# Three experts' token rows transposed by VectorE instead of TensorE, low-part products last, one conversion job moved

## The chip, the core and the metric

The kernel runs on one core of one Trainium2 chip. The metric is the device time of one execution in microseconds (us); the lower the better. Every number of the trace below comes from one profiled execution of the kernel before.

## The reference

Three layers in a row, on 2 sequences of 768 tokens with 512 features.

```python
def reference(**kwargs):
    attn_out = _attn_ref(**attn_kwargs)        # 8 heads of 64, window of 96 earlier tokens + 8 global ones, ALiBi bias
    x = attn_out.transpose(0, 2, 1, 3).reshape(B, S, H * D)
    x = _moe_ref(x=x, **moe_kwargs)            # 8 experts, each token goes to one
    return _moe2_ref(x=x, **moe2_kwargs)       # trigonometric token mixing

# expert layer, for each token: e is chosen (the gate may keep the expert of the token before it), p is a softmax of the logits
    h = np.maximum(x[b, s] @ w1[e], 0.0)       # w1: 8 x 512 x 1024
    out[b, s] = p[e] * (h @ w2[e])             # w2: 8 x 1024 x 512

# last layer
    theta = x @ w_theta
    zr, zi = x * np.cos(theta), x * np.sin(theta)
    y = np.einsum('ts,bsd->btd', w_tok_r, zr) + np.einsum('ts,bsd->btd', w_tok_i, zi)
    u = x + y
    return u + np.maximum(u @ w_ch, 0.0)
```

## The kernel before

The program is scheduled by hand: each engine executes its instructions in the order in which the Python code issues them, and an instruction that has to wait holds up all that stands behind it on its engine.

**Stages.** Attention fills the first 112 us of the span, the eight experts go from 112 to 288 us, the last layer takes the rest. The experts are sorted by their number of tokens; `r` is the place in that order. Expert `r` has room for `RCAP[r]` tokens (288, 256, 240, 208, 192, 176, 160, 144), in one tile of 128 and a remainder. The hidden width of 1024 is cut into 8 parts of 128; the loop variable `u` = 8r + f runs over all 64 parts.

**Matrix products in two parts.** Most float32 operands are split into a high part and a remainder, both in the type fp32r, and a product is made of three: high x high, high x low and low x high. The splits are made by ScalarE (the high copy, L1486 for w2, L1369 for w1) and VectorE (the subtraction, L1487, L1370). For `r` >= 4 (192 tokens or fewer, `FEW`) the first product (`mm1`, L1505) takes unsplit float32 operands and two parts of the width go together as a pair; its result passes `relu` (L1553 on ScalarE, L1554 and L1555 on VectorE). `mm2` (L1580) is split for all experts: per part `u` and tile `i` it issues hh x h2, hh x l2, hl x h2. The small remainder tiles of `r` >= 4 go through `mm2_few` (L1596). The split parts of w2, `w2s0` and `w2s1`, have three buffers each, so the split of part u + 3 needs the buffer of part u.

**Rows of an expert.** `gather_x` (L1046) fetches the rows of one tile of tokens from DRAM with one indirect DMA on GpSimd's queue, three tiles ahead. `x_tr` turns the tile: four transposes on TensorE (L1341) into PSUM, then a copy by ScalarE for `r` >= 4 (L1344). It is called for both tiles of expert r + 1 while expert r is at f = 2; for `r` >= 4 it stands between `mm1` and `mm2` of that pair. `load_piece` (L1030, L1034) fetches the weights of two parts on SyncE's queue, 512 KB for w1 and 512 KB for w2, three pairs ahead.

**Conversion jobs.** The last layer's weights come as 64-bit floats. A job converts a 128 x 512 piece in six steps, which `job_tick` issues one by one: L418 on ScalarE with L419 on VectorE, then L421, L423, L425 on VectorE, L428 on ScalarE (which also issues the load of a later piece), L431 on VectorE. There are 26 jobs. They are spread over attention, the experts (`tick`, `JRATE` is the rate per expert) and the last layer (two steps at each of three places of a block `k`: `T1`, `T2`, `T3`).

**The last layer** goes block by block of 128 tokens. For block `k` TensorE runs `h_mix(k, 0)`, `h_theta(k + 2)`, `h_mix(k, 1..3)` (L1929 and L1843). Beside it `h_tr(k + 3)` transposes the rows of a later block on VectorE (L1798), `h_xh` and `h_xl` split the result (L1814 on ScalarE, L1827 on VectorE) for `h_theta(k + 3)`, and `trig_a`, `trig_s`, `trig_b`, `trig_c` of block k + 2 make from theta (`th`) the tiles `z` that `h_mix(k + 2)` multiplies: L1853 and L1858 on ScalarE, L1860 to L1864 on VectorE, sines on ScalarE, products with the rows (L1884, L1892) and the split of `z` (L1904 on ScalarE, L1909 on VectorE). Before the loop over `k` the code runs `trig_c(1, hi)`, `h_mix(0, 3)`, then `trig_a`, `trig_s`, `trig_b`, `trig_c` of block 2. At the head of block 1, `job_upto(10)` finishes the job that is under way.

Of the kernel before, what the change touches and what calls it, by code (L numbers as in the profile page):

```python
# [12 lines left out]
I32 = mybir.dt.int32  # L13
# [38 lines left out]
VT = 2  # L52
NRAW = 3
# [21 lines left out]
JRATE = (2.0, 1.2, 1.3, 3.0, 2.7, 2.3, 0.8)  # L75
T1, T2, T3 = 2, 2, 2
# [39 lines left out]
def kernel(  # L116
# [338 lines left out]
    prow = toks.rearrange("p i w e -> p (i w e)")[:, 0:25].bitcast(I32)  # L455
    y0 = ct([128, DM], F32, "y0")
# [554 lines left out]
    def load_piece(n, parts=(1, 2)):  # L1011
# [16 lines left out]
        if 1 in parts:  # L1028
            p[1] = pre.tile([128, 4, 256], F32, tag="raw1", name="raw1", bufs=NRAW)
            SP.dma_start(  # L1030
                p[1], w1[bass.ds(ev, 1), :, c * 256 : (c + 1) * 256].rearrange("o (a p) f -> p (o a) f", p=128)
            )
# [7 lines left out]
    def gather_x(n):  # L1040
# [5 lines left out]
        G.indirect_dma_start(xg[:M], None, xd[:], bass.IndirectOffsetOnAxis(ap=xidx[:M, r, i : i + 1], axis=0))  # L1046
        xgs[n] = xg

# [275 lines left out]

    def x_tr(r, i, low=True):
# [7 lines left out]
        xg = xgs.pop(n)  # L1333

# [4 lines left out]
        M = min(128, RCAP[r] - i * 128)  # L1339
# [47 lines left out]
    with ExitStack() as mctx:  # L1387
# [179 lines left out]
        def mm2(u):  # L1567
            r, f = divmod(u, 8)
            if f == 0:
                yps[r] = [pO.tile([128, DM], F32, tag="o", name="o") for _ in range(RTILES[r] - (r == E - 1))]  # L1570
            h2, l2, w = wsp2.pop(u)
            hh, hl, hx = hts.pop(u)
            fews[u] = hx, w
            for i in range(RTILES[r]):
                lo = i * 128
                M = min(128, RCAP[r] - lo)
                if width(r, i) == 128:
                    out = yps[r][i]
                    for q, (ha, wa) in enumerate(((hh, h2), (hh, l2), (hl, h2))):
                        PE.matmul(  # L1580
                            out[:M],
                            lhsT=ha[:, lo : lo + M],
                            rhs=wa,
                            start=(f == 0 and q == 0),
                            stop=(f == 7 and q == 2),
                        )
# [79 lines left out]
        for u in range(64):  # L1666
# [41 lines left out]
            elif u % 2 == 0:  # L1708
# [7 lines left out]
                mm2(u)  # L1716
                mm2(u + 1)
# [5 lines left out]
                for _ in range(3):  # L1723
                    tick()
                relu(u + 3)
                for _ in range(3):
                    tick()
                split_w2(u + 3)
                if u == SU:
# [11 lines left out]
            if u == 1:  # L1741
                prob_rows()
            if f == (0 if r else 2):
# [21 lines left out]
    with ExitStack() as hctx:  # L1765
# [292 lines left out]
        trig_c(1, hi, V)  # L2058
        h_mix(0, 3)
# [3 lines left out]
        trig_c(2)  # L2063
# [113 lines left out]
```

## Time and profile before

| | |
|---|---|
| time, median of 3 runs | 466.54 us (466.2 to 466.86) |
| time of the profiled execution | 466.93 us |
| its span, first to last instruction | 465.0 us |
| granted TensorE clock over the span | 0.999 |
| TensorE busy | 457.9 us (98%) |
| VectorE, ScalarE, GpSimd busy | 344.0, 262.3, 142.9 us |

The span is what the trace shows; the time holds 1.9 us more around it. Engines are PE (TensorE matmuls), PEld (its weight loads), DVE (VectorE), ACT (ScalarE), POOL (GpSimd) and SP (SyncE). In a timeline each row has a start in us from the span's beginning, a duration in us, the engine, the line of the code, the operation, the tiles written and read, the shape and a count; a bracket tells how long the engine was idle before it and what ended that.

### The profile page before, as it was taken

Reading aid. Unit: us, or ns where it says so; the run is one execution under the profiler, and the core shown is the slowest. Engines: PE = TensorE matmul, PEld = TensorE weight load, DVE = VectorE, ACT = ScalarE, POOL = GpSimd, SP = SyncE. Lnnn points to the kernel's source line nnn. Section 1 sums busy time; section 2 is a strip of 40 time slices with the busy share of each in tenths; the row PEclk is TensorE's granted clock in tenths of the full one; section 3 lists DMA queues with packets and bytes.
Section 4 is the critical chain, followed back from the end, with each engine's and each line's share of the span. In section 5 each row is a group of like instructions: output and inputs, shape, how many; then the busy total and the mean of one; then the engine's idle time right before and its main releaser. Section 6 shows DMA issues by size and latency. Waiting matters only on the chain.

```text
span 465.0 us, 9578 instructions
## 1 busy us (share of the span) xinstructions
PE 457.9 (98%) x3346; PEld 378.7 (81%) x3346; DVE 344.0 (74%) x946; ACT 262.3 (56%) x623; POOL 142.9 (31%) x203
## 2 busy tenths in 40 slices
PE   8999999999999999999999999999999999999996
PEld 4677777788888898888787788888888888888886
DVE  5888889768687697887888776687997897741522
ACT  5988786822456666655755544556765665630300
POOL 8602313204032404040514302654874441000400
PEclk9999999999999999999999999999999999999999
DMA  8978577715957788788999993521253110000022
GB/s 241 367 231 248 184 240 253 252 47 158 356 167 225 265 296 270 257 277 270 318 348 307 305 312 132 165 91 48 79 152 109 43 49 24 0 35 34 28 87 93
DMA packets 61770, 85.60 MB, mean 184 GB/s; under 512 B 6248, under 2 KB 40296, under 8 KB 61720
## 3 DMA queue, kind: packets, MB, share of 16 engines
q1 hardware_dynamic: 52212, 62.06, 40.8%
q0 software_dynamic: 5552, 12.55, 8.8%
q10 hardware_dynamic: 3956, 10.36, 6.6%
q8 instruction: 27, 0.44, 0.4%
q14 instruction: 23, 0.19, 0.1%
HBM read 73.56 MB, written 11.38 MB: 183 GB/s over the span
## 4 chain that ended last, share of the span: by engine, by line
PE 90%; ACT 4%; DVE 3%; issue 1%; DMA 1%; POOL 0%; DVEq 0%
PE a L1929 22%; PE o L1580 15%; PE h L1524 10%; PE h L1505 8%; PE b L1966 7%; PE th L1843 7%; PE s L574 4%; PE x L653 3%; PE o L1596 3%; PE pt L629 3%; ACT pr L606 2%; PE tr L1341 1%; PE y L670 1%; DVE sm L596 1%; ACT ps L638 1%; PE h L783 1%
## 5 line engine op out<-in xcount | busy, mean ns | idle before, releaser
L1929 PE MATMUL a<-wtokr,z 128*128 128x512 f32 x480 | 85.3, 336 | 0.0
L1929 PEld LDWEIGHTS a<-wtokr,z 128*128 128x128 f32 x480 | 74.2, 188 | 10.0
L1580 PE MATMUL o<-w2s,hh 128*128 128x512 f32 x192 | 62.7, 406 | 0.0
L606 ACT ACTIVATE pr<-sm,st 128x256 f32<-128x256 f32 (+1 forms) x96 | 46.0, 483 | 15.3 <-DVE st L596 15.2
L1524 PE MATMUL h<-xT,w1s 128*128 128x288 f32 (+3 forms) x384 | 51.4, 284 | 0.5 <-DVE xT L1347 0.5
L1524 PEld LDWEIGHTS h<-xT,w1s 128*128 128x128 f32 x384 | 48.7, 189 | 3.4 <-issue 0.6
L1783 POOL DMA_INDIRECT xq<-yd,Lall x40 | 42.4, 1059 | 25.2 <-issue 9.8
L1487 DVE TENSOR_TENSOR w2s<-raw,w2s 128x512 fp32r<-128x512 f32 x56 | 38.5, 689 | 8.4 <-ACT w2s L1486 8.4
L596 DVE CUSTOM_DVE_ANT_0 sm<-s,bias 128x256 f32<-128x256 f32 (+1 forms) x96 | 34.0, 395 | 9.2 <-PE s L574 5.1
L1505 PEld LDWEIGHTS h<-xT,raw 128*128 128x128 f32 x256 | 37.0, 190 | 4.4 <-issue 3.9
L1505 PE MATMUL h<-xT,raw 128*128 128x192 f32 (+3 forms) x256 | 40.5, 311 | 0.0
L1580 PE MATMUL o<-w2s,hl 128*128 128x512 f32 x96 | 38.0, 396 | 0.0
L1580 PEld LDWEIGHTS o<-w2s,hh 128*128 128x128 f32 x192 | 32.4, 184 | 5.8 <-DVE w2s L1487 1.0
L1486 ACT ACTIVATE w2s<-raw 128x512 fp32r<-128x512 f32 x56 | 34.8, 626 | 2.9 <-DMA raw<-in_w_dram 1.4
L1635 POOL DMA_DIRECT2D yd<-yo x13 | 8.2, 634 | 79.1 <-ACT yo L1631 72.4
L1974 DVE SCALAR_TENSOR_TENSOR ob<-b,xTf 128x512 f32<-128x512 f32 (+1 forms) x16 | 8.8, 558 | 29.0 <-PE b L1966 25.7
L1370 DVE TENSOR_TENSOR w1s<-raw,w1s 128x512 fp32r<-128x512 f32 x32 | 22.0, 689 | 6.9 <-ACT w1s L1369 6.4
L574 PE MATMUL s<-kall,q 64*128 64x256 f32 (+1 forms) x192 | 26.1, 391 | 0.0
L629 PE MATMUL pt<-ident,pr 128*128 128x128 f32 x176 | 24.6, 278 | 0.2
L653 PE MATMUL x<-ps,vv 128*64 128x128 f32 x352 | 24.5, 279 | 0.0
L428 ACT ACTIVATE wtokr<-jw 128x512 fp32r<-128x512 f32 x15 | 9.5, 633 | 24.6 <-DVE jw L425 24.6
L1843 PE MATMUL th<-wth,xh 128*128 128x512 f32 x88 | 22.4, 396 | 0.0
(294 smaller groups left out, 944.3 us busy)
## 6 DMA issues: line engine op xcount, KB each, us to landing
raw<-in_w_dram SPq DMA_DIRECT2D x60, 512.0 KB, 5.4
vv<-in_pack_dram SPq DMA_DIRECT2D x10, 512.0 KB, 6.5
jraw<-in_w_tokT_dram ACTq DMA_DIRECT2D x10, 512.0 KB, 5.0
w<-in_w_dram SPq DMA_DIRECT2D x16, 256.0 KB, 5.4
kall<-in_pack_dram SPq DMA_DIRECT2D x10, 320.0 KB, 5.3
xd<-xt SPq DMA_DIRECT2D x12, 256.0 KB, 2.3
q<-in_pack_dram SPq DMA_DIRECT2D x11, 256.0 KB, 4.4
jraw<-in_w_tokT_dram ACTq DMA_DIRECT2D x10, 256.0 KB, 4.7
```

The costliest lines, as they stand in the source:

```text
L574: PE.matmul(sp[hh][:, 0:W], lhsT=qs[n][half, j], rhs=kall[half, b, j, t * 160 + 160 - W : t * 160 + 160], start=True, stop=True,)
L596: V.tensor_tensor_reduce(out=sm[:, hh, 0:W], in0=ust[u]["s"][hh], in1=bias[:, 2 * j + hh], scale=-0.125, scalar=BIG, op0=ALU.add, op1=ALU.min,
L606: A.activation(pr[:, hh, 0:W], sm[:, hh, 0:W], AF.Exp, bias=st[:, hh : hh + 1], scale=-1.0, accum_out=sums[n][:, 2 * j + hh : 2 * j + hh + 1],
L629: PE.transpose(pt[:, hh, c], pr[:, hh, c * 128 : (c + 1) * 128], ident)
L653: PE.matmul(xp[64 * hh : 64 * hh + 64, j], lhsT=vv[:, i, h * 64 : (h + 1) * 64], rhs=ps[:, hh, c], start=(c == 0), stop=(c == nch - 1),)
L1487: V.tensor_tensor(l2, bb[:, o], f32(h2), op=ALU.subtract)
L1505: PE.matmul(hp[:, :N], lhsT=pieces[u // 2][1][:, j, o * 128 : (o + 1) * 128], rhs=x[:, j, :N], start=(j == 0), stop=(j == 3),)
L1524: PE.matmul(hp[:, :N], lhsT=wa[:, j], rhs=xa[:, j, :N], start=(k == 0), stop=(k == 11))
L1580: PE.matmul(out[:M], lhsT=ha[:, lo : lo + M], rhs=wa, start=(f == 0 and q == 0), stop=(f == 7 and q == 2),)
L1783: G.indirect_dma_start(xq[:, i * 128 : (i + 1) * 128], None, yd.rearrange("n (q w) -> (n q) w", q=4), bass.IndirectOffsetOnAxis(ap=yq[:, i ...
L1843: PE.matmul(th, lhsT=xa[:, j], rhs=wa[:, j], start=(n == 0), stop=(n == 11))
L1929: PE.matmul(acc[b][d][o], lhsT=za[:, d * 128 : (d + 1) * 128], rhs=wa[:, lo:hi], start=(t == 0 and n == 0 and (o == 0 or d % 2 == 0)), sto ...
```

## The change

1. **Rows of experts 5, 6 and 7** (`VX` = 5). Four new tables of row numbers (`quarters`, in parts u = 2 to 5) let `gather_x` fetch quarters of rows, 128 pieces of 512 bytes at a time, so that 32 tokens' four quarters lie on the four groups of 32 partitions. A tile of 128 tokens takes four indirect DMAs, the remainders of 48, 32 and 16 tokens two, one and one. `x_tr` is then one VectorE transpose of 32 x 32 blocks into the place that ScalarE's copy filled, whose input is read with a step of 4 elements. The order of features in it is 4p + j, and w1 is loaded in the same order.
2. **`mm2`**: for `r` < 4 the high products of all tiles come first, then hh x l2, then hl x h2. For `r` >= 4 it takes both parts of a pair: hh x h2 of u, of u + 1, then the low ones of u, then those of u + 1.
3. **Steps around `relu`** for `r` >= 4: 2 ticks, `relu`, 2 ticks, `split_w2(u + 3)`, 2 ticks, in place of 3 ticks, `relu`, 3 ticks, `split_w2(u + 3)`.
4. **Jobs**: lower rates for `r` = 3 to 6; three job steps before `h_mix(0, 3)` and three after `trig_c(2)`, ahead of the loop of the last layer; one more step in each of its blocks 1 to 4; `job_upto` of blocks 1 to 5 becomes an assertion at build time.

```diff
-JRATE = (2.0, 1.2, 1.3, 3.0, 2.7, 2.3, 0.8)
-T1, T2, T3 = 2, 2, 2
+JRATE = (2.0, 1.2, 1.3, 2.9, 2.4, 2.0, 0.7)
+T0, T1, T2, T3 = 5, 2, 2, 2
...
-            SP.dma_start(
-                p[1], w1[bass.ds(ev, 1), :, c * 256 : (c + 1) * 256].rearrange("o (a p) f -> p (o a) f", p=128)
-            )
+            order = "o (a p) f -> p (o a) f" if r < VX else "o (p a) f -> p (o a) f"
+            SP.dma_start(p[1], w1[bass.ds(ev, 1), :, c * 256 : (c + 1) * 256].rearrange(order, p=128))
...
-        G.indirect_dma_start(xg[:M], None, xd[:], bass.IndirectOffsetOnAxis(ap=xidx[:M, r, i : i + 1], axis=0))
         xgs[n] = xg
+        if r < VX:
+            G.indirect_dma_start(xg[:M], None, xd[:], bass.IndirectOffsetOnAxis(ap=xidx[:M, r, i : i + 1], axis=0))
+            return
+
+        for k in range(-(-M // 32)):
+            idx = xq[:, k, r - VX, i : i + 1] if k < 2 else xq2[:, k - 2, r - VX : r - VX + 1]
+            G.indirect_dma_start(
+                xg[:, k * 128 : (k + 1) * 128],
+                None,
+                xd.rearrange("n (q w) -> (n q) w", q=4),
+                bass.IndirectOffsetOnAxis(ap=idx, axis=0),
+            )
...
+    def quarters(q):
+
+        o = slice(32 * q, 32 * q + 32)
+        for k in range(4):
+            p = slice(32 * k, 32 * k + 32)
+            dst, src = (xq[o, k, 0 : E - VX], xidx[p, VX:E, 0:2]) if k < 2 else (xq2[o, k - 2, 0 : E - VX], xidx[p, VX:E, 0])
+            V.tensor_scalar(dst, src, 4.0, float(q), op0=ALU.mult, op1=ALU.add)
+
     def x_tr(r, i, low=True):
...
         xg = xgs.pop(n)
+        M = min(128, RCAP[r] - i * 128)
+        if r >= VX:
+            k = -(-M // 32)
+            V.transpose(
+                f32(xh[:, :, i * 128 : i * 128 + 32 * k]).rearrange("p j (k a) -> p k j a", a=32),
+                xg[:, 0 : 128 * k].rearrange("p (k c j) -> p k j c", c=32, j=4),
+            )
+            gather_x(n + 3)
+            return
 
         if r > 1 and i:
...
-        def mm2(u):
-            r, f = divmod(u, 8)
+        def mm2(*us):
+
+            r, f = divmod(us[0], 8)
             if f == 0:
                 yps[r] = [pO.tile([128, DM], F32, tag="o", name="o") for _ in range(RTILES[r] - (r == E - 1))]
-            h2, l2, w = wsp2.pop(u)
-            hh, hl, hx = hts.pop(u)
-            fews[u] = hx, w
-            for i in range(RTILES[r]):
-                lo = i * 128
-                M = min(128, RCAP[r] - lo)
-                if width(r, i) == 128:
-                    out = yps[r][i]
-                    for q, (ha, wa) in enumerate(((hh, h2), (hh, l2), (hl, h2))):
-                        PE.matmul(
-                            out[:M],
-                            lhsT=ha[:, lo : lo + M],
-                            rhs=wa,
-                            start=(f == 0 and q == 0),
-                            stop=(f == 7 and q == 2),
-                        )
+            prods = [[], [], []]
+            for u in us:
+                h2, l2, w = wsp2.pop(u)
+                hh, hl, hx = hts.pop(u)
+                fews[u] = hx, w
+                for i in range(RTILES[r]):
+                    if width(r, i) == 128:
+                        c = slice(i * 128, min(i * 128 + 128, RCAP[r]))
+                        out = yps[r][i][: c.stop - c.start]
+                        prods[0].append((out, hh[:, c], h2, u % 8 == 0, False))
+                        low = [(out, hh[:, c], l2, False, False), (out, hl[:, c], h2, False, u % 8 == 7)]
+                        for k in range(2):
+                            prods[1 if len(us) > 1 else 1 + k].append(low[k])
+            for out, ha, wa, first_, last_ in prods[0] + prods[1] + prods[2]:
+                PE.matmul(out, lhsT=ha, rhs=wa, start=first_, stop=last_)
...
-                mm2(u)
-                mm2(u + 1)
+                mm2(u, u + 1)
...
-                for _ in range(3):
+                for _ in range(2):
                     tick()
                 relu(u + 3)
-                for _ in range(3):
+                for _ in range(2):
                     tick()
                 split_w2(u + 3)
+                for _ in range(2):
+                    tick()
...
+            if u in range(2, 6):
+                quarters(u - 2)
...
         trig_c(1, hi, V)
+        job_tick(3)
         h_mix(0, 3)
         trig_a(2)
         trig_s(2)
         trig_b(2)
         trig_c(2)
+        job_tick(3)
         for k in range(1, NB):
             b, t = divmod(k, NT)
             last = t == NT - 1
             if k < NT:
-                job_upto(7 + 3 * k)
+                assert jstate["k"] >= 7 + 3 * k and not (jstate["k"] == 7 + 3 * k and jstate["gen"])
...
-            job_tick(T1)
+            job_tick(T1 + (k < T0))
...
```

## Rows read from the trace of the kernel before

**Rows 1.** The page's first part: busy us of each engine, share, instructions.

```profile
PE 457.9 (98%) x3346; PEld 378.7 (81%) x3346; DVE 344.0 (74%) x946; ACT 262.3 (56%) x623; POOL 142.9 (31%) x203
```

**Rows 2.** Stretches: length, busy us (instructions) PE, PEld, DVE, ACT, POOL, clock, DMA, GB/s.

```profile
215.00:259.00 44.00, 44.00 (x267) 34.51 (x266) 37.01 (x78) 26.59 (x54) 12.83 (x18) 1.00 0.95 315
...
312.00:334.00 22.00, 22.00 (x120) 18.99 (x120) 17.90 (x31) 14.47 (x26) 13.21 (x12) 1.00 0.23 62
```

**Rows 3.** Timeline of PE, pairs of experts 4 (221 to 232) and 6.

```profile
221.05 2.87 PE L1505 MATMUL h<-xT,raw 128*128 128x192 f32 x16
223.75 0.98 PE L1341 MATMUL tr<-ident,xg 128*128 128x128 f32 x8
...
227.27 2.87 PE L1505 MATMUL h<-xT,raw 128*128 128x192 f32 x16
229.84 0.76 PE L1580 MATMUL o<-w2s,hh 128*128 128x512 f32 x2
...
232.47 2.65 PE L1505 MATMUL h<-xT,raw 128*128 128x176 f32 x16
...
262.54 2.44 PE L1505 MATMUL h<-xT,raw 128*128 128x160 f32 x16
...
267.85 2.44 PE L1505 MATMUL h<-xT,raw 128*128 128x160 f32 x16
...
272.18 2.23 PE L1505 MATMUL h<-xT,raw 128*128 128x144 f32 x16
```

**Rows 4.** Groups of DVE by form: count, busy us, mean ns of one, idle.

```profile
L1798 DVE STREAM_TRANSPOSE xTf<-xq 128x512 f32<-128x512 f32 x10 | 7.1, 706 | 0.3 <-DMA xq<-yd,Lall 0.3
...
L254 DVE TENSOR_REDUCE Lall<-lh 128x9 f32<-128x72 f32 x12 | 3.4, 284 | 0.4
...
L1406 DVE TENSOR_SCALAR Lall<-yidx 32x10 int32<-32x10 int32 x16 | 2.6, 163 | 0.2
```

**Rows 5.** Timeline of DVE: the w2 split of part 36.

```profile
226.33 0.69 DVE L1487 TENSOR_TENSOR w2s<-raw,w2s 128x512 fp32r<-128x512 f32 x1 [0.22 <-ACT w2s L1486]
```

**Rows 6.** The page's groups: POOL's indirect DMAs of 128 x 128 pieces.

```profile
L1783 POOL DMA_INDIRECT xq<-yd,Lall x40 | 42.4, 1059 | 25.2 <-issue 9.8
```

**Rows 7.** Timeline, parts 0 and 1: weight loads that waited for DVE.

```profile
119.36 0.19 PEld L1580 LDWEIGHTS o<-w2s,hh 128*128 128x128 f32 x1 [0.23 <-DVE w2s L1487]
...
121.01 0.19 PEld L1580 LDWEIGHTS o<-w2s,hh 128*128 128x128 f32 x1 [0.42 <-DVE w2s L1487]
```

**Rows 8.** Timeline, last pair: split of part 63, and PE around it.

```profile
285.53 0.40 PE L1580 MATMUL o<-w2s,hl 128*128 128x512 f32 x1
...
285.96 0.64 ACT L1486 ACTIVATE w2s<-late 128x512 fp32r<-128x512 f32 x1 [0.30 <-PE o L1580]
...
286.48 0.71 PE L1580 MATMUL o<-w2s,hh 128*128 128x512 f32 x2
```

**Rows 9.** Timeline of DVE, last layer: end of z(1) to h_tr(4).

```profile
311.66 0.42 DVE L1909 TENSOR_TENSOR z<-kk,z 128x256 fp32r<-128x256 f32 x1
312.81 0.69 DVE L1860 SCALAR_TENSOR_TENSOR rr<-kk,th 128x512 f32<-128x512 f32 x1 [0.72 <-ACT kk L1858]
...
318.68 0.69 DVE L1909 TENSOR_TENSOR z<-kk,z 128x512 fp32r<-128x512 f32 x1 [0.16 <-ACT z L1904]
...
321.28 0.71 DVE L1798 STREAM_TRANSPOSE xTf<-xq 128x512 f32<-128x512 f32 x1
```

**Rows 10.** Timeline of ACT, same stretch.

```profile
311.53 0.58 ACT L1853 ACTIVATE kk<-th 128x512 f32<-128x512 f32 x1
...
320.01 0.63 ACT L428 ACTIVATE wtokr<-jw 128x512 fp32r<-128x512 f32 x1 [1.36 <-DVE jw L425]
...
322.02 0.63 ACT L1814 ACTIVATE xh<-xTf 128x512 fp32r<-128x512 f32 x1 [0.23 <-DVE xTf L1798]
```

**Rows 11.** Timeline of PE, same stretch: where h_mix(2) and h_theta(4) start.

```profile
315.66 8.49 PE L1929 MATMUL a<-wtokr,z 128*128 128x512 f32 x48
323.99 2.02 PE L1843 MATMUL th<-wth,xh 128*128 128x512 f32 x8
```

More of the change, by code (lines that the diff above doesn't have):

```diff
@@ L52 @@
 VT = 2
+VX = 5
 NRAW = 3
@@ L455 @@
     prow = toks.rearrange("p i w e -> p (i w e)")[:, 0:25].bitcast(I32)
+    xq = toks.rearrange("p i w e -> p (i w e)")[:, 25:41].bitcast(I32).rearrange("p (k r i) -> p k r i", k=2, i=2)
+    xq2 = toks.rearrange("p i w e -> p (i w e)")[:, 41:49].bitcast(I32).rearrange("p (k r) -> p k r", k=2)
     y0 = ct([128, DM], F32, "y0")
@@ L1338, in x_tr @@
             tp = (pR_[0] if r else pZ).tile([128, 4, 128], F32, tag="tr", name="tr")
-        M = min(128, RCAP[r] - i * 128)
         for j in range(4):
```

## The prediction

> **What bounds the kernel now.** I read the page's busy times first: TensorE works for 98% of the span, no other engine for more than 74% [rows 1]. Then the stretches: in experts 4 to 6 TensorE is busy for all of 44.0 us, and for all of 22.0 us at the start of the last layer, at full granted clock [rows 2]. So only two things move the end: TensorE instructions that go away, and waits that open in its queue. The second column to watch is the one next to full: the DMA engines at 0.95 in experts 4 and 5, and VectorE at 17.9 of 22.0 us in the last layer [rows 2]. Last I read timelines, to see how far each operand is ready ahead of its use.
>
> **Part 1, the transposes.** In expert 4 a pair with the 8 transposes of the next expert's two tiles lasts from 221.05 to 227.27, 6.22 us; the next pair, with the same instructions but those, from 227.27 to 232.47, 5.20 us. In expert 6 it is 5.31 (262.54 to 267.85) against 4.33 us (to 272.18) [rows 3]. So the transposes cost 1.02 and 0.98 us; for expert 5 I take the mean. Their removal for experts 5, 6 and 7 gives **-3.0 us**, all of it on the path, as TensorE never idles there. ScalarE loses the six copies behind them.
>
> In their place VectorE gets six transposes. A 128x512 one takes 0.71 us where its input is contiguous [rows 4]. Here the input has a step of 16 bytes; the nearest row with a step (36 bytes) is a reduction of 72 elements in 284 ns, 3.9 ns per element with its fixed cost in it [rows 4]. The two tiles of expert 5 (512 and 256 elements) thus take between 1.1 and 3.0 us; I take 1.1, since it is the same operation. They stand in VectorE's queue ahead of the w2 split of part 36, which was done at 227.02 and needed after 229.84, 2.8 us later [rows 5, 3]. Up to that the cover holds, beyond it every microsecond is one of TensorE. I count 0, with 0.2 per expert as the upper end. The transposes depend on gathers issued an expert earlier, so I expect no wait for them.
>
> GpSimd issues 16 gathers where it issued 6: 10 x 1.06 us [rows 6]. It is busy for 12.8 of 44.0 us [rows 2], and what queues behind them (row probabilities, stores of the last expert's output) is wanted only an expert later. Cost 0. The 16 index instructions (0.16 us each, by a like one [rows 4]) put 0.65 us on VectorE in each of parts 2 to 5; 0 taken, up to 0.4 in the range. The new order of w1's rows moves pieces of the same length; 0.
>
> **Part 2, the order of products.** The number of matmuls stays. In parts 0 and 1 the weight load for hh x l2 waited 0.23 and 0.42 us for VectorE [rows 7]; with the other tile's high product ahead of it, most of that is covered. A load overlaps the matmul before it, so I take **-0.3 us**, between -0.65 and 0. On the other side, the buffer of h2 comes free one product later. This matters where a split waits for it: ScalarE's split for part 63 waited for the product that started at 285.53, began at 285.96 and took 0.64 us [rows 8]. One product later it ends near 286.8, and in the new order it is wanted right after the first product of the last pair, which started at 286.48 [rows 8]. I count **+0.1 us**, up to 0.3. The steps around `relu` hide behind TensorE.
>
> **Part 3, the job.** Six rates and ticks worked through by hand: the experts lose 7 job steps of six to a job, so job 17 is a third done when they end, where job 18 was half done. All 7 are made up by block 4. The last layer's own weights are still ready in time: the last table is due at block 5.
>
> The cost is in where they stand. Three steps (two of VectorE, then ScalarE's copy L428) now lie between the end of z(1) at 312.08 and `trig_a(2)`. ScalarE began `trig_a(2)` at 311.53 [rows 9, 10]. Now L428 stands ahead of it and must wait for two VectorE steps of about 0.7 us each: 312.1 + 1.4 = 313.5, then 0.63 for L428 itself [rows 9, 10], so `trig_a(2)` begins near 314.1, 2.5 us later. VectorE's rr moves from 312.81 to 315.3, and z(2) from 319.37 to 321.9 [rows 9]. `h_mix(2)` begins after 36 of the 48 matmuls that run from 315.66 to 323.99, near 321.9, and takes the last part of z(2) over a microsecond later [rows 11]: just in time. Behind z(2) the three further steps replace the three that `job_upto` put there, at about the same length, so `h_tr(4)` comes about 2.3 us later than 321.28 [rows 9]. ScalarE's xh(4) then ends near 324.9 instead of 322.65 [rows 10], and `h_theta(4)` wants it at 323.99 [rows 11]. The slack was 1.34 us, the delay 2.2 to 2.6: TensorE waits **+1.0 us**. The bounds are 0 (VectorE has holes of 0.72 and more there [rows 9]) and 3.5, if none of the replaced steps counts. After that VectorE, with 7 steps per block, again runs faster than TensorE, and nothing else is late.
>
> **Sum.** -3.0 - 0.3 + 0.1 + 1.0 = -2.2 us. The traced execution took 466.93 us for a span of 465.0; the same change to it gives a span near 462.8. From the median of 466.54 I predict **464.3 us**.
>
> **The rivals.**
> - *No wait in the last layer.* The job's steps fall into VectorE's holes, or xh(4) comes earlier. For it: VectorE is idle for 4 of 22 us there [rows 2]. Against: ScalarE's queue, not VectorE, passes the delay on. It gives 466.54 - 3.2 = 463.3.
> - *The gain is eaten elsewhere.* The DMA engines, at 0.95 in experts 4 and 5 [rows 2], set the pace: 44.0 us at 315 GB/s are 13.9 MB; less 0.4 MB of job loads, at the same rate, 42.6 us, where 42.0 are wanted. With 0.6 us lost there and a wait of 2 us in the last layer: 465.9. For it: the share. Against: no matmul of `mm1` waits for a piece in the pairs read.
> - *VectorE's transposes are slow, and the kernel slower.* At twice the row's 3.9 ns per element, 7.8 ns, the pairs of tiles (768, 640 and 640 elements) take 6.0, 5.0 and 5.0 us; less the cover of 2.8 us, TensorE waits 3.2 + 2.2 + 2.2 = 7.6 us, which gives 471.9. It turns slower than before by more than noise from 3.8 us for a pair on. For it: no row has this step. Against: it would need 3.5 times the contiguous price. [...]
> - *Nothing happens*: the freed time turns into waits for the splits, which VectorE and ScalarE make at their old pace: 466.5. Against: w2's splits are done 2.8 us ahead [rows 5, 3].
>
> **How the numbers follow.** Forecast 0.60, no wait 0.17, eaten 0.13, slow transposes 0.05, nothing 0.05. A change under 0.2% (0.93 us) is not told from none by a measurement of this kernel. Faster by more, below 465.6: the forecast (0.58 of its 0.60, the rest where its wait is over 2 us), no wait, and some of the eaten case: 0.80. Within: 0.14. Slower: 0.06. The range goes from 463.0, the no-wait case with the full 0.65 of the products' waits, to 465.9, the eaten case: it leaves out the slow, the unmoved and some edges, under 0.2 together.
>
> **What would show it.** In the trace after: no L1341 above expert 4, and in experts 4 to 6 the pair that had the transposes as long as the next (5.2, 5.0, 4.3 us). A STREAM_TRANSPOSE of xT at 0.7 us; over 2 us speaks for the third rival. An idle of about 1 us of PE or PEld ahead of L1843 near 321 (324 less the 3 us gained), ended by ACT L1814: none speaks for the first. L1487 ending the weight loads' waits of part 36, 44 or 52 would mean that the cover is gone; a wait of `mm1` for a DMA, the second. The prediction is wrong if the transposes' time on TensorE comes back as waits in the same pair, or the last layer waits in more than one place.

## The result, and the profile after

The changed kernel takes **470.76 us** (median; 469.73 to 472.82) against 466.70 us for the kernel before beside it: ratio 1.0092 [1.0069, 1.0116]. In a second comparison it is 1.0108 [1.0084, 1.0131] (471.03 against 466.68 us). The forecast was 464.3 us. The kernel is slower, by some 4 us.

The page of the changed kernel, busy us of each engine (the execution shown, the slowest of its six at 472.82 us, has a span of 471.0 us):

```profile
PE 458.7 (97%) x3321; PEld 378.3 (80%) x3322; DVE 350.8 (74%) x968; ACT 259.8 (55%) x617; POOL 152.2 (32%) x213
```

Against [rows 1] TensorE works as long as before, though it lost 24 transposes. The stretches of [rows 2], and two more at the end (length, busy us of PE, PEld, DVE, ACT, POOL, clock, DMA share, GB/s):

```profile
215.00:259.00 44.00, 43.67 (x258) 34.22 (x259) 38.60 (x79) 24.95 (x49) 17.47 (x21) 1.00 0.94 310
312.00:334.00 22.00, 20.79 (x112) 17.69 (x111) 17.74 (x30) 13.94 (x24) 11.91 (x12) 1.00 0.24 66
...
355.60:358.20 2.60, 0.96 (x6) 0.56 (x4) 2.11 (x4) 1.18 (x3) 1.99 (x3) 1.00 0.32 99
358.20:365.10 6.90, 5.95 (x17) 4.88 (x18) 6.72 (x12) 4.59 (x8) 2.61 (x3) 0.52 0.34 104
```

TensorE is no longer full in the first two stretches, VectorE has 1.6 us more in the first, GpSimd 4.6 us more. The last ran at a granted clock of 0.52 (called half clock below); in the stretch ahead of it TensorE was busy for 0.96 of 2.60 us. The pairs that [rows 3] showed, on PE's timeline of the changed kernel (start, length):

```profile
221.71 2.87 PE L1537 MATMUL h<-xT,raw 128*128 128x192 f32 x16
...
226.92 2.87 PE L1537 MATMUL h<-xT,raw 128*128 128x192 f32 x16
...
261.39 2.44 PE L1537 MATMUL h<-xT,raw 128*128 128x160 f32 x16
265.74 2.44 PE L1537 MATMUL h<-xT,raw 128*128 128x160 f32 x16
270.07 2.23 PE L1537 MATMUL h<-xT,raw 128*128 128x144 f32 x16
```

The pair with the transposes lasts 5.21 us instead of 6.22, in expert 6 4.35 instead of 5.31: they are gone, at their price. What came in their place, the group on VectorE by form (count, busy us, mean ns), beside the contiguous one of [rows 4]:

```profile
L1361 DVE STREAM_TRANSPOSE xT<-xg 128x512 f32<-128x512 f32 x3 | 3.3, 1110 | 0.1
...
L1833 DVE STREAM_TRANSPOSE xTf<-xq 128x512 f32<-128x512 f32 x10 | 7.0, 704 | 0.6 <-DMA xq<-yd,Lall 0.6
```

And TensorE's waits in the changed kernel (what it waited for, us, times, longest), first those of 196 to 300 us, then those of 318 to 372:

```profile
PE o L1618 <- DVE w2s L1519: 0.6, 1, 0.6
PE o L1618 <- DVE hl L1587: 0.3, 1, 0.3
...
PE a L1964 <- DVE wtokr L434: 2.6, 1, 2.6
PE th L1878 <- ACT xh L1849: 1.2, 1, 1.2
```

**Where the time went.** I take the distances between the first `mm2` products of one expert and the next (expert 7: from the start of its first product to the start of its last), and those between the first `h_mix` products of the blocks, from the traces:

```
us                    exp 4-5  5-6    6-7    7      blocks 2-3  5-6     ratio to before
before                21.53   20.53  17.91   9.45   11.13      11.13
after                 21.02   19.75  16.94  10.79   12.61      16.79    1.0092
after again           21.01   19.82  17.47  11.00   12.63      14.01    1.0108
e1_old_jobs           21.33   20.93  17.23  10.98   (11.13)    (11.13)  1.0032
e2_jobs_only          22.01   20.54  17.91  9.72    (11.69)    (14.01)  1.0104
e3_transposes_only    21.66   21.07  16.94   9.94   (11.13)    (11.13)  1.0046
e4_products_only      21.39   20.53  17.91   9.67   (11.13)    (11.13)  0.9986
e5_row_order_only     21.53   20.53  17.91   9.51   (11.13)    (11.13)  0.9997
e6 .._old_order       21.67   21.05  16.91  10.32   (11.13)    (11.13)  1.0045
e9_scalar_copies      20.67   20.53  16.94  10.22   11.13      11.13    0.9977
e10_gathers_only      21.52   20.54  17.91   9.45   11.13      11.13    1.0026
e11_one_expert        21.41   20.53  16.94  10.42   11.13      11.13    1.0002
e12_two_experts       21.49   20.24  17.27   9.67   11.83      12.01    1.0014
e13 one, no jobs      21.42   20.53  16.94   9.67   -          -        -
e14 all, no jobs      20.53   19.55  16.94   9.66   -          -        -
e15 jobs from exp. 6  21.40   20.34  18.23   9.67   12.75      12.03    1.0053
e16 jobs to exp. 1    21.04   19.55  16.94   9.67   11.19      11.13    0.9992
e7_job_phases         20.99   19.96  16.94   9.99   (11.13)    (11.79)  0.9992
e7_again              21.02   19.88  16.94   9.77   13.40      12.02    1.0014
```

On two of the chips (runs e1 to e6 and e7_job_phases, before 479.1 to 479.5 us) every kernel, that of before too, takes 16.8 to 18.0 us instead of 6.4 from the first `h_theta(0)` to `h_mix(0)`. I take it that the job then has room ahead of block 1, so their last layers (in brackets) are not compared with the others'. In experts 4 to 7 the kernel before, traced on one of them, has the same 21.51, 20.53, 17.91 and 9.45 us.

In the changed kernel experts 4 to 6 give -2.3 us of the 3.0 (in the second trace -1.7), expert 7 gives 1.3 (1.6) of that back, and the last layer loses 1.5 us at `h_theta(4)` and 2.9 at `h_mix(5)`, 5.7 where the half clock follows.

These figures vary with one and the same schedule. e7_again and e7_job_phases issue the experts exactly as the changed kernel does; they lose 0.3 and 0.5 us in expert 7 and not 1.3 and 1.6, and e7_job_phases alone loses 1.5 us between the first products of experts 3 and 4.

### The profile page after: what moved, and what is told of

Its sections match the earlier page's. It is cut to its first block, busy times and chain, and to the rows that moved or that the text cites. A ratio compares the mean times of both kernels' runs of the same rounds, so it can differ in the third digit from the quotient of the medians.

```text
span 471.0 us, 9561 instructions
## 1 busy us (share of the span) xinstructions
PE 458.7 (97%) x3321; PEld 378.3 (80%) x3322; DVE 350.8 (74%) x968; ACT 259.8 (55%) x617; POOL 152.2 (32%) x213
## 4 chain that ended last, share of the span: by engine, by line
PE 69%; DVE 10%; ACT 7%; DMA 6%; issue 4%; POOL 2%; ACTq 0%; DVEq 0%; SPq 0%; POOLq 0%
PE a L1964 13%; PE o L1618 12%; PE h L1556 9%; PE b L2001 7%; PE h L1537 6%; PE s L580 4%; PE th L1878 3%; PE x L659 3%; PE pt L635 3%; PE o L1628 2%; DMA late<-in_w_dram 2%; ACT pr L612 2%; POOL xq L1818 1%; PE y L676 1%; PE small L883 1%
## 5 line engine op out<-in xcount | busy, mean ns | idle before, releaser
L1964 PE MATMUL a<-wtokr,z 128*128 128x512 f32 x480 | 86.9, 340 | 2.6 <-DVE wtokr L434 2.6
L1964 PEld LDWEIGHTS a<-wtokr,z 128*128 128x128 f32 x480 | 75.2, 191 | 13.0 <-DVE wtokr L434 2.9
L1618 PE MATMUL o<-w2s,hh 128*128 128x512 f32 x192 | 58.2, 409 | 0.7 <-DVE w2s L1519 0.6
L1818 POOL DMA_INDIRECT xq<-yd,Lall x40 | 39.3, 983 | 30.8 <-DVE xTf L1833 14.5
L1618 PE MATMUL o<-w2s,hl 128*128 128x512 f32 x96 | 32.8, 395 | 0.3 <-DVE hl L1587 0.3
L1878 PE MATMUL th<-wth,xh 128*128 128x512 f32 x88 | 23.9, 417 | 1.2 <-ACT xh L1849 1.2
L431 ACT ACTIVATE wtokr<-jw 128x512 fp32r<-128x512 f32 x15 | 9.4, 627 | 28.4 <-DVE jw L428 28.4
```

The source lines that it names most:

```text
L1618: PE.matmul(out, lhsT=ha, rhs=wa, start=first_, stop=last_)
L1818: G.indirect_dma_start(xq[:, i * 128 : (i + 1) * 128], None, yd.rearrange("n (q w) -> (n q) w", q=4), bass.IndirectOffsetOnAxis(ap=yq[:, i ...
L1878: PE.matmul(th, lhsT=xa[:, j], rhs=wa[:, j], start=(n == 0), stop=(n == 11))
L1964: PE.matmul(acc[b][d][o], lhsT=za[:, d * 128 : (d + 1) * 128], rhs=wa[:, lo:hi], start=(t == 0 and n == 0 and (o == 0 or d % 2 == 0)), sto ...
```

## The experiments

The theories that the expectations name: **A**, all of the loss is in the job's steps in the last layer. **B**, the pieces of w1 in the new row order land late. **C**, the gathers cost what the transposes save. **D**, VectorE's waits for the job's ScalarE copy make the wait at `h_mix(5)`; **E**, seven steps per block are too many in themselves. **F**, VectorE is the bound in experts 4 and 5 once it has the transposes. **G**, the DMA engines set when the last expert's w2 is there.

**1. The parts by themselves.** `e1_old_jobs` is the changed kernel without the job's part:

```
-JRATE = (2.0, 1.2, 1.3, 2.9, 2.4, 2.0, 0.7)
-T0, T1, T2, T3 = 5, 2, 2, 2
+JRATE = (2.0, 1.2, 1.3, 3.0, 2.7, 2.3, 0.8)
+T1, T2, T3 = 2, 2, 2
...
-        job_tick(3)          (ahead of h_mix(0, 3), and behind trig_c(2))
...
-                assert jstate["k"] >= 7 + 3 * k ...
+                job_upto(7 + 3 * k)
...
-            job_tick(T1 + (k < T0))
+            job_tick(T1)
```

`e2_jobs_only` is the kernel before with that part alone, `e3_transposes_only` with `VX`, the quartered gathers, w1's new order and VectorE's transposes alone, `e4_products_only` with `mm2(*us)` and the ticks around `relu` alone.

> The changed kernel with the conversion jobs as they were before (part 4 undone). Theory A (the loss is made by the job steps in the last layer, and the rest of the change gains): no wait ahead of h_theta(4) and none at h_mix(5), no stretch at half clock, 463.7 to 464.7 us. Theory B (the rows of experts 5 to 7 cost what they save, because the w1 pieces in the new row order land later): 465.5 us or more, with w1 landings of 8 us and waits in the experts.

> The kernel before with the job changes alone (part 4). Theory A: waits of over 1 us ahead of h_theta(4) and over 2 us at h_mix(5) for a converted table, 470 to 474 us, since here no time is gained in the experts. Theory B: under 468 us.

> The kernel before with the VectorE transposes alone (part 1). Theory A: the pair with the transposes as long as its neighbours in experts 4 to 6, 463.5 to 464.3 us. Theory B: 465.5 us or more, w1 pieces of experts 5 to 7 landing in 8 us.

> The kernel before with the new order of products and steps around relu alone (parts 2 and 3 of the list). Forecast's term: -0.2 us, 466.3 to 466.6. If the wait for hl at part 33 and the late split of parts 56 and 57, both seen in the trace after, come from it, 467 us or more.

Measured: 1.0032 [1.0018, 1.0046], 1.0104 [1.0084, 1.0123], 1.0046 [1.0031, 1.0061], 0.9986 [0.9975, 0.9996]. The job's part alone loses 5 us, with the same wait as in the changed kernel; TensorE's wait in `e2_jobs_only`, 330 to 400 us:

```profile
PE a L1929 <- DVE wtokr L431: 2.6, 1, 2.6
```

In the experts that kernel, with fewer steps of the job, is no faster than before: it takes 22.01 us from expert 4 to 5, where TensorE waits 0.3 us for VectorE's `hl`. Theory A falls: the transposes alone, which were to gain, lose 2 us. In their trace 0.8 us of it lie in experts 3 to 7, 0.6 of that between the first products of experts 3 and 4; another 0.9 us lie between blocks 4 and 5 of the last layer, where TensorE waits 0.8 us for nothing that the profile shows. None of the theories explains these two. The products' order gains a little, as forecast.

**2. Row order or not.** `e5_row_order_only` loads w1 of experts 5 to 7 in the new order and changes nothing else; `e6_transposes_old_order` is e3 with the old order:

```
-            order = "o (a p) f -> p (o a) f" if r < VX else "o (p a) f -> p (o a) f"
+            order = "o (a p) f -> p (o a) f"
```

> The kernel before with one edit: the pieces of w1 of experts 5, 6 and 7 are loaded with partition p holding rows 4p to 4p+3 instead of rows p, 128+p, 256+p, 384+p. TensorE still transposes xT; these experts then multiply rows that do not match, so their values are not the reference's, but no instruction is added or taken away and no length changes. Theory B (rows of experts 5 to 7: the new row order makes the transfers later and eats the gain of the transposes): the pieces of w1 land about 8 us after issue instead of 5.7, SP issues each in 0.55 us instead of 0.37, VectorE and ScalarE wait for raw w2 and w1 in experts 5 to 7, and the time is 1.5 to 3 us above before, ratio 1.003 to 1.006. Theory A (only the job's steps cost time): the order costs nothing that is on the path, ratio 0.999 to 1.001.

> The transposes part alone as in e3_transposes_only (VectorE transposes, quartered gathers, quarters), but the pieces of w1 keep the old row order, so experts 5 to 7 multiply rows that do not match and their values are not the reference's. Theory B: with the row order's late landings gone, the 3.0 us that TensorE no longer spends on transposes show: 2 to 3 us below before, ratio 0.9935 to 0.996, against 1.0046 with the new row order. Rival C (16 gathers on GpSimd or VectorE's transposes eat the gain): the ratio stays at 1.003 to 1.006 as in e3.

Measured: 0.9997 [0.9985, 1.001] and 1.0045 [1.0031, 1.0059]. In e5 SP does take 0.55 us for each issue, but the pieces land in 5.6 us and no stage of experts 4 to 7 moves by 0.1 us. Theory B falls; the forecast's 0 for this step was right. In the changed kernel the same pieces took up to 8.3 us, so the order is not what delays them.

**3. VectorE, or the gathers.** In `e9_scalar_copies` e3's VectorE transposes are replaced:

```
-            V.transpose(
-                f32(xh[...]).rearrange("p j (k a) -> p k j a", a=32),
-                xg[:, 0 : 128 * k].rearrange("p (k c j) -> p k j c", c=32, j=4),
+            A.activation(
+                f32(xh[...]), xg[:, 0 : 128 * k].rearrange("p (j a) -> p j a", j=4), AF.Copy
             )
```

`e10_gathers_only` keeps e3's gathers and puts `PE.transpose` back behind them (`xg[:M, j % k * 128 : (j % k + 1) * 128]`).

> The transposes part alone (as e3_transposes_only: quartered gathers, w1 in the new row order, no transposes on TensorE), but VectorE's transposes of experts 5 to 7 are replaced by ScalarE copies of the same size, so xT of these experts holds the gathered rows untransposed and their values are not the reference's. Theory F (VectorE becomes the bound in experts 4 and 5: the pairs without transposes are 1.0 us shorter on TensorE, VectorE gets 1.7 us more in the same pair, and its low parts of w2 come late): with VectorE relieved, the way from the first products of expert 4 to those of expert 7 is 57.0 to 58.5 us instead of 59.95 before and 59.6 in e3, and the time is 1 to 2.5 us below before, ratio 0.995 to 0.998. Rival C (the gathers, through GpSimd or the DMA engines, eat the gain): that way stays at 59.5 or more and the ratio at 1.003 to 1.006.

> The gathers of the transposes part alone: experts 5 to 7 are fetched in quarters of rows by 16 gathers in place of 6, with the steps that make their indices and w1 in the new row order, but TensorE transposes what lies in xg as before; the quarters are not put together rightly, so the values of experts 5 to 7 are not the reference's. Theory F: the gathers cost nothing on the path but the 0.4 to 0.6 us seen between the first products of experts 3 and 4, ratio 0.999 to 1.0015. Rival C: the loss of the transposes part shows here and is larger for the 3 us that TensorE doesn't save: ratio 1.007 or more.

Measured: 0.9977 [0.9967, 0.9986] and 1.0026 [1.0017, 1.0035]. With the transposes off VectorE the time is about 1 us below before, though ScalarE does six copies again; expert 4 to 5 falls from e3's 21.66 us to 20.67. So theory F holds for expert 4. For expert 5 e9 does not show it: 5 to 6 keeps its 20.53 us, since the first and the last pair are each 0.5 us longer than in e14 below, with w2's splits late again. Theory C is not excluded as a smaller cost: e10 is 1.1 us slower, but its trace, the fastest of its ten executions (466.91 us), shows no stage of the experts or of the last layer over 0.3 us longer than before and no wait of TensorE. Some 0.4 us of it lie outside the span: the time of e10 is 2.20 us longer than the span (e9: 2.18), that of before beside it 1.84. Where the rest is stays open.

How VectorE comes late is seen in part 37. On the timelines, before (VectorE, then PE):

```profile
228.71 0.68 DVE L1487 TENSOR_TENSOR w2s<-raw,w2s 128x512 fp32r<-128x512 f32 x1
...
230.67 0.62 PE L1580 MATMUL o<-w2s,hh 128*128 128x512 f32 x2
```

and in e6:

```profile
226.51 1.66 DVE L1361 STREAM_TRANSPOSE xT<-xg 128x512 f32<-128x512 f32 x2
...
230.25 0.68 DVE L1519 TENSOR_TENSOR w2s<-raw,w2s 128x512 fp32r<-128x512 f32 x1
...
230.98 0.50 PE L1612 MATMUL o<-w2s,hh 128*128 128x512 f32 x1 [0.56 <-DVE w2s L1519]
```

Before, the split ended at 229.39 and its low part was wanted with the second product, about 230.9: 1.5 us ahead. In e6 VectorE is 1.54 us later there and TensorE 0.64 earlier: the cover of part 37 is gone.

**4. Job steps against transposes.** `e11_one_expert` is e1 with `VX = 7`. `e13_one_expert_no_jobs` is e11, `e14_all_no_jobs` is e1, each with `JRATE = (2.0, 1.2, 1.3, 3.0, 0.0, 0.0, 0.0)`. `e12_two_experts` is `e7_job_phases` (below) with `VX = 6` and `JRATE = (2.0, 1.2, 1.3, 3.0, 2.7, 1.7, 0.5)`.

> The products part with VectorE's transposes for expert 7 alone (not 5 and 6), and the old job schedule. These transposes stand in expert 6, where VectorE has 0.8 of a job's step per slot instead of 2.3 to 2.7. Theory F: the way from the first products of expert 6 to those of expert 7 is 16.9 us instead of 17.9, no new wait in experts 4 and 5, and with the products' gain the time is 1 to 2 us below before, ratio 0.996 to 0.998. If the transposes cost the same wherever they stand, the ratio is 0.9985 to 1.0005.

> The changed kernel with the job's steps placed as in e7_job_phases, VectorE's transposes for experts 6 and 7 only, and the steps that leave the experts taken from expert 5 and 6 alone (rates 3.0, 2.7, 1.7, 0.5 for experts 3 to 6), where these transposes stand. Theory F: expert 4 to 5 takes 21.4 us, expert 5 to 6 19.5 instead of 20.5, expert 6 to 7 16.9 instead of 17.9; the last layer is as in e7_job_phases, up to 1.0 us later than before; sum 1 to 1.5 us below before, ratio 0.996 to 0.999. If the job's steps do not matter for what the transposes cost, expert 5 to 6 stays at 20.5 or more and the ratio is 1.000 or more.

> e11_one_expert with no step and no table load of the job in experts 4 to 6; the steps that are left out there are made up at the start of the last layer, which is longer for it, so only the stages up to the last product of expert 7 are compared. Theory G (the DMA engines set when the last expert's w2 is there): with some 4 MB of table loads gone from these 70 us, the last expert's w2 lands within 6.5 us of its issue, and expert 7 takes 9.3 to 9.6 us from its first to its last product instead of 10.4 in e11, while expert 6 to 7 keeps its 16.9. If the transposes have a fixed cost at the end of the experts, it stays at 10.2 or more.

> The changed kernel's transposes (experts 5, 6, 7) and products, with no step and no table load of the job in experts 4 to 6; these are made up at the start of the last layer, which is longer for it, so only the stages up to the last product of expert 7 are compared. Theories F and G together (VectorE in experts 4 and 5, the DMA engines at the end): expert 4 to 5 takes 20.5 us (21.53 before), 5 to 6 19.5 (20.53), 6 to 7 16.9 (17.91), expert 7 9.3 to 9.6 (9.45): the forecast's 3.0 us are there. If one of these stays as in e3_transposes_only (21.66, 21.07, 16.94, 9.94), the cause there is another (the gathers).

Measured: e11 1.0002 [0.9994, 1.0011], e12 1.0014 [1.0004, 1.0024]; e13 and e14 by their stages alone. In e11 expert 6 to 7 has its 16.94 us and nothing new waits in experts 4 and 5, as theory F has it, but expert 7 gives 0.97 back and the first product behind the experts waits 0.5 us for gathered rows, so the ratio is that of the other branch. e12 misses too: expert 5 to 6 gains 0.3 us and not 1.0, and the last layer loses 1.6. Its pair with the transposes does get 1.0 us shorter, but the pairs at the turn to expert 6 are 0.7 and 0.3 us longer, where TensorE waits 0.4 us for ScalarE's `hh`; and it waits 1.2 us for gathered rows ahead of `h_mix(0)`. The first ScalarE step on the last expert's w2, before, in the changed kernel, in e11, e13, e14 and e7_again:

```profile
275.01 0.63 ACT L1486 ACTIVATE w2s<-late 128x512 fp32r<-128x512 f32 x1 [2.77 <-DMA late<-in_w_dram]
...
275.01 0.63 ACT L1518 ACTIVATE w2s<-late 128x512 fp32r<-128x512 f32 x1 [4.65 <-DMA late<-in_w_dram]
...
275.21 0.63 ACT L1518 ACTIVATE w2s<-late 128x512 fp32r<-128x512 f32 x1 [2.58 <-DMA late<-in_w_dram]
...
273.82 0.63 ACT L1518 ACTIVATE w2s<-late 128x512 fp32r<-128x512 f32 x1 [2.46 <-DMA late<-in_w_dram]
...
271.61 0.63 ACT L1518 ACTIVATE w2s<-late 128x512 fp32r<-128x512 f32 x1 [2.66 <-DMA late<-in_w_dram]
...
273.33 0.63 ACT L1518 ACTIVATE w2s<-late 128x512 fp32r<-128x512 f32 x1 [3.64 <-DMA late<-in_w_dram]
```

In the first three it stands at 275.0 to 275.2, whether TensorE is 2 us ahead or not. SP issued that load at 265.6, 264.6, 265.2, 266.2, 263.8 and 264.0: it took 9.4, 10.4, 10.0, 7.6, 7.8 and 9.4 us to ScalarE's step. The stretches of expert 6, first products to first products, in e11 and e13:

```profile
259.60:276.50 16.90, 16.90 (x154) 13.94 (x153) 12.20 (x34) 7.50 (x16) 5.28 (x7) 1.00 1.00 318
...
260.60:277.50 16.90, 16.90 (x154) 13.94 (x153) 10.58 (x33) 7.52 (x15) 5.58 (x7) 1.00 0.85 269
```

With the job's tables out of the way the DMA engines fall from 1.00 to 0.85, the load takes 2.4 us less, and expert 7 its 9.67 us (the products' order makes 9.67 of 9.45, see e4). So theory G holds as far as the load goes, and all twenty traces say by how much: expert 7 takes 9.45 us (9.67 with the new order of products), and longer by what that ScalarE step falls short of 2.3 us ahead of the first product. It stands 3.3 us ahead before, 1.2 in the changed kernel (1.0 in its second trace), 1.5 in e11, 3.9 in e13 and 2.2 in e7_again, which thus loses almost nothing.

The share of the DMA engines does not order the load's times: from its issue to the step it is 0.91 in the kernel before, with 9.4 us, and 0.92 in e13, with 7.6. What does is a table load of the job beside it. Where none is issued within 6 us of it (e13, e14 and e15) it takes 7.6 to 8.0 us; in the other traces one or two are issued within 4 us, and it takes 8.9 to 11.1.

In e14 both bounds are off, and all three experts give the forecast's gain: 1.00, 0.98 and 0.97 us. It takes the job's steps off VectorE and ScalarE and its loads off the DMA engines at once, so by itself it does not tell F from G.

**5. The job's steps in the last layer.** `e7_job_phases` keeps the changed kernel's seven steps per block and moves them among the block's three places:

```
-T0, T1, T2, T3 = 5, 2, 2, 2
+STEPS = {1: (3, 2, 2), 2: (1, 3, 3), 3: (1, 3, 3), 4: (3, 2, 2)}
...
-            job_tick(T1 + (k < T0))
+            job_tick(STEPS.get(k, (2, 2, 2))[0])
...
```

> The changed kernel with the same number of job steps in each block of the last layer, but placed 3,2,2 / 1,3,3 / 1,3,3 / 3,2,2 at the three places of blocks 1 to 4 instead of 3,2,2 in each, so that the job's ScalarE copy (L431) no longer stands behind the four sine instructions while VectorE's next step (L434) waits for it. Theory D (in blocks 2 and 3 VectorE waits about 2 us each for that copy; this delay, not the count of steps, makes the wait of 2.8 us for the converted table at h_mix(5) and the stretch at half clock behind it): the waits of L434 fall below 0.5 us, h_mix(5) waits under 0.5 us, the distance from block 5's to block 6's products is about 11.2 us instead of 16.8, and the time is 4 to 6 us below the changed kernel's: against before 1.000 to 1.004 (the transposes part alone stood at 1.0032 with products, and the wait of about 1.4 us for h_theta(4) stays). Rival E (the seven steps per block themselves are too many for VectorE): the wait at h_mix(5) stays above 1.5 us and the ratio is 1.007 or more.

> The kernel of e7_job_phases again: the changed kernel with its job steps in blocks 1 to 4 of the last layer placed 3,2,2 / 1,3,3 / 1,3,3 / 3,2,2. Theory D (VectorE's waits for the job's ScalarE copy make the wait at h_mix(5)): the wait at h_mix(5) is under 1.0 us instead of 2.8, no stretch at half clock follows, the wait for h_theta(4) stays at 1.2 to 1.6 us, and the time is 2 to 4 us below the changed kernel's 1.009 to 1.011: ratio 1.001 to 1.006.

VectorE's waits for the job's ScalarE copy in the last layer, before (from 310 us to 372) and in the changed kernel (from 318):

```profile
DVE wtokr L431 <- ACT wtokr L428: 0.7, 1, 0.7
...
DVE wtokr L434 <- ACT wtokr L431: 4.3, 2, 2.5
```

In the changed kernel that copy (L431) stands behind the four steps of `trig_s` on ScalarE (L1906 to L1911: two sines, a square and a copy). VectorE's rows, then ScalarE's, then the table's last step and the products that want it:

```profile
337.74 0.69 DVE L434 TENSOR_TENSOR wtokr<-jw,wtokr 128x512 fp32r<-128x512 f32 x1 [1.87 <-ACT wtokr L431]
...
348.68 0.69 DVE L434 TENSOR_TENSOR wtokr<-jw,wtokr 128x512 fp32r<-128x512 f32 x1 [2.46 <-ACT wtokr L431]
...
345.65 0.63 ACT L1906 ACTIVATE si<-rr 128x512 f32<-128x512 f32 x1 [1.12 <-DVE rr L1899]
347.50 0.63 ACT L1911 ACTIVATE kk<-kk 128x512 f32<-128x512 f32 x1
348.04 0.61 ACT L431 ACTIVATE wtokr<-jw 128x512 fp32r<-128x512 f32 x1
...
358.41 0.69 DVE L434 TENSOR_TENSOR wtokr<-jw,wtokr 128x512 fp32r<-128x512 f32 x1
...
359.15 1.22 PE L1964 MATMUL a<-wtokr,z 128*128 128x256 f32 x3 [2.59 <-DVE wtokr L434]
```

VectorE's turn per block is 10.94 us in the blocks with such a wait (`h_tr` at 332.21, 343.15, 354.09), where it was 8.83 before and a seventh step adds about 0.6. PE's waits in e7_again, 318 to 372 us:

```profile
PE th L1878 <- ACT xh L1849: 2.0, 1, 2.0
PE a L1964 <- DVE wtokr L434: 0.6, 1, 0.6
```

Measured: 0.9992 [0.9981, 1.0002], and 1.0014 [1.0003, 1.0025] beside e16. VectorE's waits for L431 are gone, the wait at `h_mix(5)` falls from 2.6 to 0.6 us, no half clock follows, and the time falls by 0.8 to 0.9% against the changed kernel's two ratios. Seven of that kernel's ten executions have a granted clock of 0.993 to 0.996 over the span; all twelve of e7_again have 0.999 or 1.000. Theory D holds for the wait and the half clock, E falls. Not all of the time is the phases': of the 3.2 us between the traces of after_again and e7_again 1.9 lie ahead of the last layer, where the two issue the same (neither trace has the half clock). The wait for `h_theta(4)` was expected at 1.2 to 1.6 us and is 2.0.

**6. Other places for the job.** `e15_jobs_from_expert6` is e7_job_phases with `JRATE = (2.0, 1.2, 1.3, 3.0, 2.6, 2.3, 0.0)`; `e16_jobs_to_expert1` is e1 with `JRATE = (2.0, 2.0, 1.4, 3.0, 2.3, 1.9, 0.7)`, the last layer as before. Beside e15 ran the changed kernel again.

> The changed kernel with the job's steps in the last layer placed as in e7_job_phases and the steps that leave the experts taken from expert 6 (rate 0) and a little from expert 4 (2.6 instead of 2.7), not spread over experts 3 to 6. Theory G: without table loads in expert 6 the last expert takes 9.3 to 9.7 us (10.8 in the changed kernel, 10.0 in e7_job_phases); theory F: expert 4 to 5 and 5 to 6 keep most of VectorE's delay (21.3 to 21.6 and 20.3 to 21.0). Sum of the experts 0.5 to 1.5 us below before, the last layer up to 1.0 above: ratio 0.998 to 1.001.

> The changed kernel itself, for its ratio on the same chip as e15. All theories: 1.007 to 1.012, with the wait of some 2.8 us for the converted table at h_mix(5) and, behind it, a stretch at half clock.

> The changed kernel's transposes (experts 5, 6, 7) and products, the last layer's job steps as in the kernel before, and the same number of job steps in the experts, but 6 to 7 of them moved from experts 4 and 5 (and 1 from 6) to experts 1 and 2 (rates 2.0, 2.0, 1.4, 3.0, 2.3, 1.9, 0.7 in place of 2.0, 1.2, 1.3, 3.0, 2.7, 2.3, 0.8). Theories F and G: expert 1 and 2 keep their 23.06 and 22.6 us, expert 4 to 5 takes 20.6 to 21.1 us (21.53 before), 5 to 6 19.6 to 19.9 (20.53), 6 to 7 16.9 (17.91), expert 7 9.7 to 10.8 (9.45); the last layer is that of before; the time is 1 to 2 us below before, ratio 0.995 to 0.998. If the transposes have a cost of another kind (gathers, w1's order), the ratio is 1.000 or more.

Measured: 1.0053 [1.0041, 1.0065], 1.0108 and 0.9992 [0.9983, 1.0001]. e15 misses: expert 7 is short (9.67) as expected, but expert 6 to 7 waits 1.3 us for w2's splits, and the last layer loses 2.5 us. In e16 the experts gain as expected (21.04, 19.55, 16.94; 2.4 us), but expert 1, to which most of the steps went, takes 24.71 us instead of 23.06: VectorE was busy for 16.8 of 23 us there before, and in e16's trace TensorE waits 0.5 us for its splits of w1. Expert 0, whose rate is unchanged, takes 30.10 us in this trace (29.06 in the changed kernel), the slowest of eleven executions, and loses that microsecond before the first step of the job is issued, so this part is not the moved steps'. Gain and loss are nearly equal again.

The fastest kernel that leaves nothing out is e4, the products' order alone, at 0.9986 of before; with VectorE's transposes none was faster than before by more than 0.1%.

## Why the prediction was wrong

Two steps failed: the cover that was to hide VectorE's transposes, and the sentence that nothing else is late in the last layer. A third term, the DMA engines in the experts, was put at nothing and cost 1 us.

**Transposes, -3.0: the size right, the step to the end wrong.** e14 shows 2.95 us. The step that failed is the cover: "They stand in VectorE's queue ahead of the w2 split of part 36 ... 2.8 us later. Up to that the cover holds." I priced VectorE's two tiles at 1.1 us with 1.1 to 3.0 as bounds; they take 1.67, within the bounds. But I measured the cover at one split [rows 5, 3] and left out two things: the next split, of part 37, had 1.5 us and not 2.8, and each microsecond that TensorE saves is taken from the same cover. With VectorE at 37.0 of 44.0 us [rows 2] there was little idle time in which it could catch up, and the old job rates kept it late (e3 21.66 and 21.07 us). The change's lower rates do pay for that (21.02 and 19.75), at the price of the last layer.

**Nothing else is late in the experts: wrong for the DMA engines.** The row that I named, 0.95 in experts 4 and 5 [rows 2], was a bound; I gave it 0.13 as the rival "eaten elsewhere", and looked for it as a wait of `mm1`. It shows as the time at which the last expert's w2 is there: 1.3 and 1.6 us lost in expert 7, of which 0.2 is the products' (e4, e13: 9.67), and 0.3 in e7_again, where the load came sooner.

**Products, -0.3 and +0.1.** Expert 0 to 1 takes 29.06 us instead of 29.32, -0.26 [rows 7]; expert 7 in e4 +0.22 [rows 8]. The h2 buffer cost twice what I took, within its bound of 0.3. e4 as a whole is 0.14% faster, 0.6 us, with the forecast's 0.2 at the edge of its interval.

**The job, +1.0: mechanism right, size short.** The chain of [rows 9 to 11] in the changed kernel, VectorE, ScalarE, then PE:

```profile
314.66 0.69 DVE L1895 SCALAR_TENSOR_TENSOR rr<-kk,th 128x512 f32<-128x512 f32 x1 [1.85 <-ACT kk L1893]
...
320.54 0.69 DVE L1944 TENSOR_TENSOR z<-kk,z 128x512 fp32r<-128x512 f32 x1 [0.16 <-ACT z L1939]
...
323.00 0.70 DVE L1833 STREAM_TRANSPOSE xTf<-xq 128x512 f32<-128x512 f32 x1
...
312.85 0.63 ACT L431 ACTIVATE wtokr<-jw 128x512 fp32r<-128x512 f32 x1 [1.82 <-DVE jw L428]
313.39 0.58 ACT L1888 ACTIVATE kk<-th 128x512 f32<-128x512 f32 x1
...
323.73 0.63 ACT L1849 ACTIVATE xh<-xTf 128x512 fp32r<-128x512 f32 x1 [1.51 <-DVE xTf L1833]
...
324.42 2.13 PE L1878 MATMUL th<-wth,xh 128*128 128x512 f32 x8 [1.21 <-ACT xh L1849]
```

Step by step as forecast (L431 ahead of `trig_a(2)`, rr, z(2), `h_tr(4)`), with the layer begun 0.8 us earlier; the loss is 1.5 us, within the bounds 0 to 3.5. It varies: the same three steps ahead of the loop go with 0.7 us there in e12 and 2.3 in e7_again.

**"After that VectorE, with 7 steps per block, again runs faster than TensorE, and nothing else is late": the costliest error,** 2.9 us and up to 5.7. I counted steps (8.83 + 0.6 us is indeed less than TensorE's 11.13) and did not follow which step of the six falls at which place. Six steps per block put the copy each time where VectorE hardly waited for it (0.7 us in all between 310 and 372 us of the kernel before); seven shift it by one place per block, until it stands behind the four steps of `trig_s`. The copy's operand was ready at 343.23 us (L428, 342.54 + 0.69), ScalarE then stood idle for 1.12 us ahead of L1906, and still the copy began only at 348.04, 0.54 us after the last of these steps had begun, with VectorE waiting 2.46 us.

**The rivals.** Slow transposes did not come: 1.11 us against 0.70 for the contiguous form, a factor of 1.6 and not 3.5. Both write the same layout, so the step of the input is what differs. "Nothing happens" came near the truth for e11 and e16 (e3 is slower by 2 us): the freed time turned into waits, for splits above all, which I had weighed at 0.05 by the cover of one part.

## What to carry to other kernels

Work that is moved to an engine with idle time can be paid twice in cover: that engine's results come later (1.54 us in e6), and the engine that was relieved asks for them earlier (0.64 us); measure the slack of every result that follows until the next real gap, not of the first. Filler work that advances by a fixed number of steps per round has a phase against the other engines' queues: when the number changes, follow each kind of step to its new place before counting it as free (VectorE waited 0.7 us for the copy with six steps per block, 4.3 with seven). A load that lands just ahead of its use can be a bound for whoever comes to it earlier, even where nobody waits for it now (the last expert's w2: its first step 3.3 us ahead before, 1.2 in the changed kernel, and expert 7 1.3 us longer).

## What the runs showed that I had not expected

- The wait of 2.59 us at `h_mix(5)`, from 356.56 to 359.15, ran into a clock of 0.52 from 358.2 on over 6.9 us in one trace of the changed kernel; in the second a wait of 2.61 us passed at full clock; the way to block 6 is 16.79 us in the one and 14.01 in the other. So the same schedule has two prices.
- w1's rows in the new order cost SP 0.55 us per issue instead of 0.37, and nothing else (5.6 us to landing in e5).
- Between chips, the same kernel differs by 12 us (466.7 and 479.1 us), nearly all of it ahead of `h_mix(0)`.
